# Where q of a later unit is asked for, and the order of one unit's attention, in a fused attention and feed-forward kernel

## The chip, the cores and the metric

The kernel runs on one core of a Trainium2 chip. The metric is the device time of one execution in microseconds. Before the change it is 909.99 us, the median of three runs (909.27 to 911.45).

## The reference

What is computed, with batch 8, 8 heads, 576 positions, 64 dimensions per head, and a feed-forward width of 2048:

```python
kv = np.einsum('bhsd,bhse->bhde', k, v)
out = np.einsum('bhsd,bhde->bhse', q, kv)
rms = np.sqrt(np.mean(out * out, axis=-1, keepdims=True) + 1e-06)
x = (out / rms * g_norm)            # then heads side by side: 4608 x 512
h = x @ w_in                        # 512 x 2048
r = np.maximum(h, 0.0)
g = s * (r * r) + b
return g @ w_out                    # 2048 x 512
```

All of it is in float32.

## The kernel before

**Units.** The 4608 rows of x are cut into 36 blocks of 128 rows, and four blocks make a unit; the code counts units from 0 to 8. In each unit the kernel multiplies the unit's x by `w_in` (`mm1`, or `mm1_deep` from unit 2 on), applies the activation, and multiplies by `w_out` (`mm2`). Both products use Winograd's form of the seven-product scheme for 2 x 2 blocks, at one or two levels. This needs sums and differences of blocks of x, of the weights and of the activations, which VectorE makes.

**Attention of the next unit.** While unit u is computed, the attention of unit u + 1 is made beside it, in two pairs of blocks, A and B. `attention_of_two` (L516) cuts each pair into steps: `turn` (VectorE transposes q, L540), `product` (64 or 32 small matmuls with k^T v on TensorE, L552), `back` (two VectorE transposes out of PSUM into the q tile, L564), `square` (ScalarE), `row_sum` (VectorE and ScalarE), `norm` (VectorE reads the q tile for the last time, L583 and L585), `turn_x` (VectorE, L596) and `scale` (ScalarE). `kv_product` (L365) makes k^T v of a batch: 144 matmuls, and four ScalarE copies (L400) into one of two tiles `bd_kv`. With its second argument true, it uses one PSUM bank each of the tags `z` and `y`; otherwise two of the tag `t`.

**The order is written out by hand.** The kernel schedules manually: each engine runs its instructions in the order in which the code emits them. In units 0 and 1, the second product is a list of slots, and `side_of` (L1628) says which steps follow which slot. In units from 2 on, `run` in `mm1_deep` (L947) calls `at(n)` between its pieces, and `sides` (L1718) gives two dictionaries: `first` for these places, and `second` for the places in `rest` (L1405) of `mm2`. At the beginning of `run` stand, in this order: `x1(0)`, `at(2)`, `x1(1)`, `sums_of_x` (four VectorE differences into two tiles of the pool `sub`), `small(2,0,1,2)`, `x6(0)`, `at(4)`, `at(5)`, `small(2,0,6,7)`, `y7(0)`, `at(6)`, `small(2,0,5)`. A `small` piece has short matmuls, each followed by a VectorE addition (L260 or L267) that reads the bank `sx_ps` or `z_ps`. The next matmul into `sx_ps` needs the addition before it.

**q tiles.** There are two of them (pool `qp`, two buffers). `load_q(c)` (L132) takes a tile for the pair of blocks c and c + 1 and returns the loads as a list; for the pair 14, the second half of unit 3, which is the fourth unit, it is 16 loads of 32 KB with runs of 32 floats. `loads` (L1651) issues them all at once on POOL's queue (L1655). A tile may be overwritten only after `norm` of the pair that it held.

**Weights and k, v.** SP loads pieces of the weights and of k and v into `ring`, 14 places of one tile, in the order of `queue_w2`; `used` frees places, and `pump` (L1063) then sends what fits. k and v of a unit stand ahead of its weights and take eight places.

**Stores of weight sums.** In unit 1, `parts_of_w` (L1130) makes the sums of each of the seven parts of `w_out` in tiles of the pool `sub` (six buffers, and two more for one of them) and stores them by four POOL DMAs (L1145) to `w3_dram`. These run in the even slots. Output stores (L1248) are on POOL too. So POOL's queue in the second half of unit 1 is: stores of parts 1, 2, 6, 7, 5; then 16 loads of q; then four output stores; stores of part 3; eight output stores; stores of part 4; four output stores.

The few lines that set this order before the change:

```python
            6: [B["norm"]],
            8: [B["turn_x"], B["scale"]],
            11: [sums],
            9: [partial(loads, 3, 1)],
```

## Time and profile before

| | us |
|---|---|
| median of three runs | 909.99 |
| the profiled execution | 909.79 |
| its span, from the first to the last instruction | 908.0 |
| PE busy (TensorE matmul) | 892.4 |
| DVE busy (VectorE) | 683.4 |
| ACT busy (ScalarE) | 345.5 |
| POOL busy (GpSimd) | 261.5 |

The durations in what follows come from the profiled execution. PE is a queue of 7662 matmuls; a matmul row's end is modelled, so the start of the next row tells more than a row's length. Idle time before an instruction is put down to the event that ended it. "w<-sub" is a store of weight sums from the pool `sub`; "w_sb" is the ring.

Of DMA, the page says: mean 208 GB/s over the span, and 188.77 MB in 121805 packets, of which 25456 are under 512 B. The second half of unit 1 runs from 181.37 us to 234.41 us of the span, unit 2 from there to 338.04 us.

### The profile page before, as it was taken

How to read it: one execution, taken by the hardware profiler on the slowest of the kernel's cores; microseconds unless marked ns; L12 is line 12 of the kernel's file. 1: busy time of each engine (PE TensorE's matmuls, PEld its weight loads, DVE VectorE, ACT ScalarE, POOL GpSimd, SP SyncE). 2: the span in 40 equal slices, each digit the busy share in tenths (PEclk: the TensorE clock that was granted, in tenths of full speed). 3: DMA queues.
4: the chain of work that ended last, by engine and by line, in shares of the span. 5: the costliest groups of instructions: out<-in, count | busy, mean ns of one | idle time of the engine just before them, and what ended most of it. 6: DMA issues, size and time to landing. Idle time of an engine off the chain costs nothing.

```text
span 908.0 us, 19742 instructions
## 1 busy us (share of the span) xinstructions
PE 892.4 (98%) x7662; PEld 825.4 (91%) x7662; DVE 683.4 (75%) x1321; ACT 345.5 (38%) x584; POOL 261.5 (29%) x493
## 2 busy tenths in 40 slices
PE   7999999999899999999999999999999999999998
PEld 6888888888789998999899989999999989999998
DVE  2899687785467986787678877796779777974696
ACT  2887024531057204640266026701661056204610
POOL 2027067023713415610473036503430200021000
PEclk9999999999999999999999999999999999999999
DMA  9897649359842996379735983498539921892186
GB/s 254 312 331 232 194 107 286 132 135 361 258 143 80 290 323 193 83 230 311 239 83 178 316 289 81 126 321 268 149 92 302 303 58 60 290 304 80 58 278 187
DMA packets 121805, 188.77 MB, mean 208 GB/s; under 512 B 25456, under 2 KB 43248, under 8 KB 121712
## 3 DMA queue, kind: packets, MB, share of 16 engines
q1 hardware_dynamic: 101744, 161.65, 55.1%
q0 software_dynamic: 16512, 23.63, 9.3%
q10 hardware_dynamic: 3456, 2.23, 1.0%
q8 instruction: 61, 1.00, 0.5%
q14 instruction: 32, 0.26, 0.1%
HBM read 160.70 MB, written 26.74 MB: 206 GB/s over the span
## 4 chain that ended last, share of the span: by engine, by line
PE 83%; DVE 6%; issue 4%; DMA 3%; POOL 2%; ACT 1%; SPq 0%; DVEq 0%; POOLq 0%
PE x_ps L92 40%; PE y_ps L92 22%; PE z_ps L92 10%; PE sx_ps L92 6%; PE st_ps L92 2%; PE y_ps L552 2%; DMA w<-sub 1%; POOL w L1145 1%; DMA kv_sb<-in_v_dram 1%; DMA q_sb<-in_q_dram 1%; PE kv_ps L384 1%; DVE sub L263 1%; PE z_ps L384 1%; DVE a L263 1%; POOL q_sb L1655 1%
## 5 line engine op out<-in xcount | busy, mean ns | idle before, releaser
L1655 POOL DMA_DIRECT2D q_sb<-in_q_dram x312 | 175.8, 571 | 127.1 <-issue 68.4
L1248 POOL DMA_DIRECT2D out_dram<-o x120 | 59.4, 502 | 324.9 <-issue 164.2
L92 PE MATMUL x_ps<-w_sb,sub 128*128 128x128 f32 x1176 | 148.8, 276 | 1.1 <-DVE r L260 1.0
L92 PEld LDWEIGHTS x_ps<-w_sb,sub 128*128 128x128 f32 x1176 | 139.7, 192 | 1.5 <-DVE r L260 1.5
L651 ACT ACTIVATE a<-a,b_col,s_col 128x512 f32<-128x512 f32 x144 | 116.9, 813 | 25.8 <-DVE a L654 17.6
L848 ACT COPY a<-x_ps 128x512 f32<-128x512 f32 x28 | 16.3, 581 | 232.0 <-PE x_ps L92 231.9
L92 PE MATMUL y_ps<-xs,wb 128*128 128x256 f32 x416 | 99.3, 382 | 0.0
L92 PE MATMUL x_ps<-xs,ws_raw 128*128 128x256 f32 x384 | 91.1, 380 | 0.1
L92 PEld LDWEIGHTS y_ps<-xs,wb 128*128 128x128 f32 x416 | 77.1, 192 | 9.2 <-issue 0.2
L92 PE MATMUL x_ps<-xT,wa 128*128 128x256 f32 x360 | 84.1, 382 | 0.1
L92 PEld LDWEIGHTS x_ps<-xs,ws_raw 128*128 128x128 f32 x384 | 70.1, 191 | 8.6 <-ACT r L725 0.5
L92 PEld LDWEIGHTS x_ps<-xT,wa 128*128 128x128 f32 x360 | 66.7, 190 | 10.6 <-ACT a L944 1.3
L944 ACT ACTIVATE a<-a 128x512 f32<-128x512 f32 x112 | 69.5, 620 | 5.5 <-DVE a L267 5.5
L92 PE MATMUL x_ps<-w_sb,a 128*128 128x128 f32 (+1 forms) x432 | 64.9, 299 | 0.0
L92 PE MATMUL y_ps<-w_sb,a 128*128 128x128 f32 (+1 forms) x416 | 62.2, 295 | 0.0
L92 PEld LDWEIGHTS x_ps<-w_sb,a 128*128 128x128 f32 x432 | 58.4, 192 | 2.9 <-issue 0.4
L92 PEld LDWEIGHTS y_ps<-w_sb,a 128*128 128x128 f32 x416 | 56.1, 192 | 2.1
L260 DVE TENSOR_TENSOR r<-sx_ps,a 128x256 f32<-128x256 f32 x84 | 35.1, 418 | 26.2 <-PE sx_ps L92 25.7
L260 DVE TENSOR_TENSOR r<-x_ps,o 128x256 f32<-128x256 f32 (+1 forms) x84 | 29.7, 353 | 27.7 <-PE x_ps L92 27.0
L92 PE MATMUL y_ps<-w_sb,sub 128*128 128x128 f32 x392 | 49.5, 275 | 0.0
L92 PE MATMUL z_ps<-w_sb,a 128*128 128x128 f32 (+1 forms) x352 | 46.9, 280 | 0.0
L263 DVE TENSOR_TENSOR a<-a,a 128x512 f32<-128x512 f32 x72 | 46.7, 684 | 0.1
(221 smaller groups left out, 1593.4 us busy)
## 6 DMA issues: line engine op xcount, KB each, us to landing
w_sb<-w SPq DMA_DIRECT2D x413, 256.0 KB, 4.8
w_sb<-w SPq DMA_DIRECT2D x14, 512.0 KB, 8.7
w<-sub POOLq DMA_DIRECT2D x28, 256.0 KB, 5.4
out_dram<-o POOLq DMA_DIRECT2D x112, 64.0 KB, 3.9
w_sb<-in_k_dram SPq DMA_DIRECT2D x24, 288.0 KB, 4.4
w_sb<-in_v_dram SPq DMA_DIRECT2D x24, 288.0 KB, 4.4
w_raw<-in_moe_w_in_dram SPq DMA_DIRECT2D x6, 1024.0 KB, 7.7
q_sb<-in_q_dram POOLq DMA_DIRECT2D x160, 32.0 KB, 3.2
```

The source lines that it names most:

```text
L92: nc.tensor.matmul(o, lhsT=lhsT, rhs=rhs, start=start, stop=stop, skip_group_check=True)
L260: nc.vector.tensor_tensor(out=o, in0=a, in1=b, op=ALU.add)
L263: nc.vector.tensor_tensor(out=o, in0=a, in1=b, op=ALU.subtract)
L384: nc.tensor.matmul(ps[r][(r ^ l) * HB : (r ^ l) * HB + HB, i, :], lhsT=kv[l][0][rows, j, :], rhs=kv[l][1][rows, j, :], start=(j == 0), sto ...
L552: nc.tensor.matmul(ps[l][32 * p : 32 * p + 32, r, lo:hi], lhsT=bd_kv[b % 2][rows, p, at : at + 32], rhs=st["qT"][rows, p, lo:hi], start=Tr ...
L651: nc.scalar.activation(t, t, AF.Identity, scale=s_col, bias=b_col)
L848: nc.scalar.copy(g_tile("a11", s), st["x", s])
L944: nc.scalar.square(ga[name, s], ga[name, s])
L1145: nc.gpsimd.dma_start(out=w3_dram[i][:, m - 4], in_=t)
L1248: queues[s % 2].dma_start(out=view[b, jj, :, cols], in_=st[name, j][s * w : s * w + w, cols])
L1655: load()
```

## The change

Two things are changed.

1. In unit 1, the sixteen loads of q for the pair 14 are not issued together after slot 9. They are issued in four lots of four, after slots 7, 8, 9 and 10. The tile is taken with the first lot.
2. In unit 2, the dictionary of its own is dropped, and the one of later units is used. k^T v moves from place 6 to place 2 and uses the `z` and `y` banks; A's `turn` moves from 4 to 2, A's `product` from 7 to 4, A's `back` and `square` and B's `turn` from 8 to 5, A's `row_sum` from 9 to 6, A's `norm` from 12 to 7, A's `turn_x` from 13 to 8, A's `scale` from 16 to 11. B's `back` stays at 11; B's `square` moves from 14 to 11, and `row_sum` from 15 to 12. B's `norm` and `turn_x` move from places 1 and 2 of the second half to 13 and 14 of the first, and B's `scale` from the place "sums" of the second half to 1. The loads of q for unit 4 move from 13 and from place 3 of the second half to 10 and 15.

```diff
+        pieces = []
+
+        def ask(n):
+            if n == 0:
+                pieces.extend(load_q(14))
+            for piece in pieces[4 * n : 4 * n + 4]:
+                piece()
+
         return {
             0: [A["scale"]],
             1: [B["turn"]],
             4: [B["product"], B["back"], B["square"]],
             5: [B["row_sum"]],
             6: [B["norm"]],
-            8: [B["turn_x"], B["scale"]],
+            7: [partial(ask, 0)],
+            8: [B["turn_x"], B["scale"], partial(ask, 1)],
+            9: [partial(ask, 2)],
+            10: [partial(ask, 3)],
             11: [sums],
-            9: [partial(loads, 3, 1)],
         }
...
-            kv.append(lambda: kv_product(kv_due[u], u > 2))
+            kv.append(lambda: kv_product(kv_due[u], u > 1))
...
-        if u == 2:
-            first = {
-                4: [A["turn"]],
-                6: kv,
-                7: [A["product"]],
-                8: [A["back"], A["square"], B["turn"]],
-                9: [A["row_sum"]],
-                10: [B["product"]],
-                11: [B["back"]],
-                12: [A["norm"]],
-                13: [A["turn_x"], *q[0]],
-                14: [B["square"]],
-                15: [B["row_sum"]],
-                16: [A["scale"]],
-            }
-            second = {1: [B["norm"]], 2: [B["turn_x"]], 3: [*q[1]], "sums": [B["scale"]]}
-        else:
...
+        first = {
+            2: [A["turn"], *(kv if u in (2, 5) else [])],
+            4: [A["product"], *(kv if u not in (2, 5) else [])],
+            5: [A["back"], A["square"], B["turn"]],
+            6: [A["row_sum"]],
+            7: [A["norm"]],
+            8: [A["turn_x"]],
+            10: [B["product"], *q[0]],
+            11: [B["back"], B["square"], A["scale"]],
+            12: [B["row_sum"]],
+            13: [B["norm"]],
+            14: [B["turn_x"]],
+            15: q[1],
+        }
+        second = {1: [B["scale"]]}
```

## The prediction

> **What bounds the kernel now.** I read the page first (PE busy 98% of the span, every other engine far below), then the table of PE's waits, because an engine at 98% can only gain where it waits or runs slow. Near unit 2 it names three waits:

> ```profile
> engine line waited for: us in total, times, longest us
> PE sx_ps L92 <- DVE r L260: 3.3, 1, 3.3
> PE y_ps L552 <- DVE qT L540: 1.1, 1, 1.1
> PE x_ps L92 <- DVE r L260: 1.0, 1, 1.0
> ```

> Each occurs once, though the code in question runs seven times. So I cut the span at the first matmul of each unit and asked for the windows of units 2 to 6 (columns: PE, PEld, DVE, ACT, POOL busy with counts, granted clock, DMA share, GB/s):

> ```profile
> 234.41:338.04 103.63, 98.16 (x917) 92.07 (x916) 73.47 (x151) 35.77 (x62) 33.16 (x62) 0.98 0.68 216
> 338.04:433.49 95.45, 95.45 (x887) 90.06 (x885) 74.91 (x153) 35.45 (x62) 35.01 (x66) 1.00 0.66 211
> 433.49:529.10 95.61, 95.61 (x918) 90.46 (x917) 74.91 (x153) 35.45 (x62) 34.98 (x66) 1.00 0.67 210
> 529.10:624.91 95.81, 95.73 (x919) 90.22 (x917) 74.60 (x153) 35.45 (x62) 35.00 (x66) 1.00 0.66 210
> 624.91:720.52 95.61, 95.61 (x918) 90.64 (x917) 74.90 (x153) 35.45 (x62) 26.83 (x50) 1.00 0.66 206
> ```

> All five do the same kinds of work, a k^T v product included, yet unit 2 takes 103.63 us and the others 95.45 to 95.81. Unit 2 alone runs below full clock. The excess of about 8 us is the whole prize. The timelines of DVE and POOL show where the first wait starts:

> ```profile
> 234.61 0.42 DVE L260 TENSOR_TENSOR o<-y_ps,or 128x256 f32<-128x256 f32 x1 [0.50 <-PE y_ps L92]
> 240.19 0.42 DVE L263 TENSOR_TENSOR sub<-xT 128x256 f32<-128x256 f32 x1 [5.15 <-DMA w<-sub]
> 242.75 0.42 DVE L263 TENSOR_TENSOR sub<-xT 128x256 f32<-128x256 f32 x1 [1.68 <-DMA w<-sub]
> 243.43 0.42 DVE L260 TENSOR_TENSOR r<-sx_ps,a 128x256 f32<-128x256 f32 x1
> ```

> ```profile
> 219.83 2.20 POOL L1145 DMA_DIRECT2D w<-sub  x4 [8.17 <-DVE sub L263]
> 222.03 2.91 POOL L1655 DMA_DIRECT2D q_sb<-in_q_dram  x5
> 225.89 0.58 POOL L1655 DMA_DIRECT2D q_sb<-in_q_dram  x1 [0.95 <-DMA w<-sub]
> 227.36 0.58 POOL L1655 DMA_DIRECT2D q_sb<-in_q_dram  x1 [0.89 <-DMA w<-sub]
> 228.54 5.23 POOL L1655 DMA_DIRECT2D q_sb<-in_q_dram  x9 [0.59 <-DMA w<-sub]
> 234.31 1.99 POOL L1248 DMA_DIRECT2D out_dram<-o  x4 [0.55 <-issue]
> 236.29 2.17 POOL L1145 DMA_DIRECT2D w<-sub  x4
> ```

> DVE stands still for 6.8 us because two of the six "sub" buffers are still being stored to w3_dram[3]; those stores were issued at 236.29 only, behind sixteen q loads that held POOL from 222.03 to 233.8. Then PE waits for DVE. What follows in PE's windows (the granted clock is the third figure from the right):

> ```profile
> 244.00:245.00 1.00, 1.00 (x5) 0.50 0.53 131
> 245.00:246.00 1.00, 1.00 (x6) 0.50 0.72 262
> 246.00:247.00 1.00, 1.00 (x3) 0.50 0.90 328
> 247.00:248.00 1.00, 1.00 (x5) 0.82 0.93 332
> 248.00:249.00 1.00, 1.00 (x43) 1.00 0.97 254
> ```

> The wait is paid twice: 3.3 us of idleness, then some 3.4 us at half clock, which costs another 1.7 to 1.9 us.

> [...] 3.26 us idle, then 0.50 until about 247.4. [...] q is read here in runs of 32 floats, 128 bytes. In the trace the sixteen loads of 32 KB of the next fetch, with little beside them, took 16.8% of sixteen engines over 14 us, so 2.35 us for 0.5 MB. [...] The trace has DMA shares of 0.9 to 1.08 from 205 to 230. I find no figure for the wait of a POOL load on an earlier one; the trace shows it (the waits on w<-sub in POOL's rows above).

> **The change part by part.**

> *q of the fourth unit.* No load is added or removed; sixteen move on POOL's queue. Each takes 0.58 us to issue. Lot 1 of four (2.3 us) goes behind w7's stores, which end at 211.66, into an idle stretch of 8.17 us. It needs the old tile free: the last reader, the norm at 210.56 + 1.23 = 211.8, is just done. So it runs 211.8 to 214.1 and w5's stores still start at 219.83. Lots 2 and 3 follow w5 as the first eight loads do now, with the same three waits, and end near 229.1. Then come the first output's four stores (0.5 each) to 231.1, and w3's stores 231.1 to 233.3, instead of 236.29 to 238.46: 5.2 us earlier. Lot 4 follows, to about 235.7. Behind it stand eight output stores and w4's four, which wait for earlier landings; I estimate w4 ending near 243 instead of 246.3; nothing in the next 20 us needs it. The third w3 store, issued near 232.2, lands near 237.5 with the 5.33 us that its landing takes now (chain of waits, 237.40). DMA time is unchanged; the quarter that moves into the busy stretch before 220 is 0.6 us of sixteen engines (a quarter of 2.35). That can delay k and v by at most that. No PE time is bought directly: it brings the two buffers about 5 us earlier.

> *k^T v first, in z and y banks.* 144 matmuls, 2.28 us on PE (248.38 to 250.65), move from behind y7(0) to behind x1(0), as in unit 5 (530.83 to 533.20 there). They fill most of the time in which PE waits now. New conditions: k and v in the ring by 236.14. The last is issued at 226.39 and such loads land in 4.4 to 7.0 us, so 231 to 233.4, and 234 with the 0.6 us above: covered by 2 us. z was last read at 195.8, the y buffer at 231.6: free. ACT's four copies (1.08 us) end near 239.7, before the z bank is wanted at 240.6 and bd_kv at 242.8. The ring's eight places come free 12 us earlier, so SP sends its waiting 256 KB loads earlier (it waits 14.2 us for kv_ps now); up to 2 MB, about 6 us at 330 GB/s, start at 238.5, beside w4's stores and perhaps lot 4. By then w3's have landed.

> *Attention in the order of later units.* Operations are kept, only their places move. DVE: A's transpose (1.24) now stands ahead of x's sums, 235.0 to 236.3, in time that was idle; the sums (four, some 1.5 us with gaps) run when the buffers are free, 237.5 to 239, and r follows sx at about 241.2. PE wants both at 244.05 (234.41 + 1.73 x1 + 2.30 kv + 1.73 x1 + 0.44 + 0.45 small + 1.82 x6 + 1.20 A's product = 244.08). So the 3.26 us wait goes, and the half clock with it. Even if w3 landed at 242.75 as today, r would end at 243.8, so this part is doubly covered. What is late next: between A's product and the small product 5, DVE runs back (2 x 0.65), B's transpose (1.20) and r (0.38); PE has only 2.7 us of work there. Unit 5 has just this and shows 0.24 us (542 region: y7 ends 541.49, next starts 541.73). I take 0.24 over. B's transpose at 245.4 needs lot 4, issued by 235.7; 6.6 us is the longest landing of such a load, so 242.3. B's product then lies where later units have it without a wait (1.13 us gone). B's norm and transpose leave the second half of the unit, where they hold up DVE just before the x_ps wait: 304.20 to 307.18 takes 2.98 against 1.79 in unit 3, and a further 0.22 at 315.4 goes. Their new place in the first half is the later units' one; DVE is as busy there. The q loads of unit 4 come earlier on a POOL that idles from 248.3 to 270.0; the memsets and stores behind them are 50 us away.

> *The sum.* New unit 2 = unit 5 (95.81), plus A's product of 64 instead of 32 matmuls (1.20 against 1.03: +0.17), less B's of 32 instead of 64 (-0.07) = 95.91. Saved: 103.63 - 95.91 = 7.72. Check by places: 3.33 + 1.86 half clock + 1.20 + 1.19 + 0.3 small = 7.88, less the 0.24 of unit 5 = 7.64. The profiled execution took 909.79 (span 908.0), so 902.07; the median lies 0.2 above it: 902.2. Bounds: nothing at all of 0.24 and unit 3's 95.45 as the floor gives -8.2; one new wait of 2.5 us without a clock drop gives -5.2.

> **Rivals.**
> 1. *A remnant wait takes over*: lot 4 is slowed by SP's earlier loads, and B's transpose stands at the head of DVE with r behind it. For: in-order DVE, DMA at 1.05 in 235 to 240. Against: nearly 10 us from issue to use. Landing at 249 costs 3.6 us plus about 1.8 of half clock: 902.2 + 5.4 = 907.6; at 247, 903.8.
> 2. *Slower: k and v are late.* PE would stand at 236.14 with nothing to pass it. The gain is used up when that wait reaches 5.9 us (5.9 + 1.8 half clock = 7.7), so if v lands after 242; at 244 the kernel takes 912. Against: that is 15.6 us from the issue at 226.39, and it was 7.0 at most in this stretch, though one store reached 13.0.
> 3. *The lots do nothing* (the DMAs, not POOL's order, set w3's landing): the second cover holds, 902.5. That is in the forecast's range. That the change doesn't do what it says is excluded by the emitted order: 4, 8 and 4 loads stand on POOL around w5 and w3, and k^T v behind the first x1.

> **How the numbers follow.** Forecast 0.81 (901.2 to 903.5, rival 3 within it); remnant wait 0.11 (903.5 to 908.1); about equal 0.03; k and v late, or an unforeseen wait of that size, 0.05. A measurement of this kernel tells 0.2%, 1.8 us, from no change. Faster 0.92, same 0.03, slower 0.05. Range 900.7 to 905.0: the spread of the three runs (909.27 to 911.45) below, half of rival 1 above.

> **What would show it.** Right: unit 2 in 95.7 to 96.5 us at clock 1.00; w3's stores on POOL near 231; no PE wait over 0.5 us in unit 2; kv rows at about 236.1 without a wait. Wrong: PE waiting for a DMA at kv, DVE waiting on q_sb at B's transpose near 245, or a new wait in the second half.

## The result, and the profile after

| | before | changed |
|---|---|---|
| median, us | 909.63 (909.08 to 911.45, 4 runs) | 904.46 (903.79 to 905.29, 4 runs) |
| ratio | | 0.994, 95% interval 0.9923 to 0.9958 |
| profiled execution, us | 909.79 | 905.29 |
| its span | 908.0 | 903.5 |
| unit 2, from its first matmul to unit 3's | 103.63 | 97.72 |

The kernel is 5.2 us faster where 7.7 were forecast. In the profiled executions, unit 2 is 5.91 us shorter, it starts 1.05 us later, and what stands behind it takes 0.36 us longer (570.32 against 569.96). Sum: -4.5 of the span. The kernel before has two kinds of executions: of the 58 that ran beside the experiments below, 13 had a mean granted clock of 0.999 or 1.000 and took 907.1 to 908.4 us, and the other 45, at a lower one, took 908.2 to 912.3.

None of the three waits near unit 2 of before is left in the table of PE's waits. These are the two lines that matter, and the second is new:

```profile
PE kv_ps L384 <- DMA kv_sb<-in_v_dram: 3.5, 2, 2.5
PE z_ps L92 <- issue: 1.6, 1, 1.6
```

The first is the wait for k and v at the very start of the kernel. It was 2.1 us in the profiled execution of before, and from 0.8 to 3.5 us in the traces of this study, whatever the kernel. So the later start of unit 2 comes from this wait and not from the change. The second is put down to "issue": PE waited for nothing that the profile names. It lies in unit 2. The window of unit 2 of the changed kernel (columns as in the prediction):

```profile
235.46:333.18 97.72, 96.10 (x918) 90.44 (x916) 73.73 (x151) 35.47 (x62) 31.09 (x58) 1.00 0.69 223
```

The clock is back to 1.00 in unit 2, and PE is idle there for 1.62 us (97.72 - 96.10). POOL's timeline of the changed kernel:

```profile
220.89 2.22 POOL L1145 DMA_DIRECT2D w<-sub  x4 [5.10 <-DVE sub L263]
223.09 2.92 POOL L1646 DMA_DIRECT2D q_sb<-in_q_dram  x5
...
230.46 1.99 POOL L1248 DMA_DIRECT2D out_dram<-o  x4
232.61 1.65 POOL L1145 DMA_DIRECT2D w<-sub  x3 [0.15 <-issue]
234.50 0.54 POOL L1145 DMA_DIRECT2D w<-sub  x1 [0.25 <-issue]
235.03 2.35 POOL L1646 DMA_DIRECT2D q_sb<-in_q_dram  x4
```

Part 3's stores start at 232.61; with the 1.05 us later start of unit 2 taken off that is 231.56, against 231.1 forecast. VectorE's timeline in the same stretch:

```profile
236.00 1.24 DVE L540 STREAM_TRANSPOSE qT<-q_sb 128x1024 f32<-128x1024 f32 x1
237.16 0.38 DVE L263 TENSOR_TENSOR sub<-xT 128x256 f32<-128x256 f32 x1
...
238.23 0.42 DVE L263 TENSOR_TENSOR sub<-xT 128x256 f32<-128x256 f32 x1 [0.22 <-DMA w<-sub]
...
242.10 0.42 DVE L260 TENSOR_TENSOR r<-sx_ps,a 128x256 f32<-128x256 f32 x1 [3.11 <-PE sx_ps L92]
```

The waits for the two buffers have shrunk from 6.8 us to 0.22, and VectorE now waits for PE where PE waited for it. Both the buffers and r came within 0.4 us of the forecast, once the later start is taken off. What is left is seen in PE's timeline:

```profile
241.83 0.28 PE L92 MATMUL z_ps<-xT,wa 128*128 128x128 f32 x1
243.72 0.60 PE L92 MATMUL z_ps<-xT,wa 128*128 128x128 f32 x3 [1.61 <-issue]
```

The pause falls between two rows of one small product (a row is one matmul record of the trace). A wait for a buffer or a bank should have held the first row already, as the 3.26 us of before stood ahead of all four rows of their product (243.90). So the question for the experiments was not only whether the mechanism of the forecast is right, but what this pause is.

A theory for it came from the DMA part of the page (packets, MB, share of the sixteen engines):

```profile
q8 instruction: 61, 1.00, 0.5%
```

PE has 7662 matmul rows, 7662 loads of weights and 397 other instructions in this trace, 15721 in all; 61 packets make 258 to a packet and 64 bytes to an instruction. The packets, of 16384 bytes each, start in step with PE: from the first to the last, one in 256 PE instructions on average. So q8 most likely carries PE's own program, 16 KB at a time; this is inferred from these counts and the queue's kind. Whether the 1.61 us are a wait for such a packet was to be shown. In the changed kernel, two packets near the pause stand unusually far apart:

```
changed kernel: packet at 214.71 us, next at 241.31 us: 520 PE instructions apart; k^T v is 288 of them
kernel before:  packet at 213.77 us, next at 239.12 us: 247 PE instructions apart
```

**Theory A**: the block of program behind k^T v was asked for when k^T v began, came late, and PE ran dry. **Theory B**, its rival: the `z` bank, which the change gave to k^T v, was not free.

### The profile page after: what moved, and what is told of

The parts are those of the page before. It is cut to its first block, busy times and chain, and to the rows that moved or that the text cites. A ratio compares the mean times of both kernels' runs of the same rounds, so it can differ in the third digit from the quotient of the medians.

```text
span 903.5 us, 19737 instructions
## 1 busy us (share of the span) xinstructions
PE 889.9 (98%) x7662; PEld 823.2 (91%) x7662; DVE 683.1 (76%) x1321; ACT 345.4 (38%) x584; POOL 262.5 (29%) x493
## 4 chain that ended last, share of the span: by engine, by line
PE 93%; DVE 3%; DMA 1%; issue 1%; ACT 0%; SPq 0%; POOL 0%; DVEq 0%
PE x_ps L92 46%; PE y_ps L92 25%; PE z_ps L92 10%; PE sx_ps L92 6%; PE st_ps L92 2%; PE y_ps L552 2%; DMA kv_sb<-in_v_dram 1%; PE z_ps L384 1%; PE kv_ps L384 1%; PE y_ps L384 0%; DVE xT L596 0%; DVE xn L585 0%; DVE xs L263 0%; DVE q_sb L564 0%; DVE qT L540 0%
## 5 line engine op out<-in xcount | busy, mean ns | idle before, releaser
L1665 POOL DMA_DIRECT2D q_sb<-in_q_dram x296 | 167.1, 573 | 86.1 <-issue 44.1
L1248 POOL DMA_DIRECT2D out_dram<-o x120 | 59.5, 503 | 360.3 <-issue 211.5
L92 PE MATMUL x_ps<-w_sb,sub 128*128 128x128 f32 x1176 | 148.5, 275 | 0.0
L92 PEld LDWEIGHTS x_ps<-w_sb,sub 128*128 128x128 f32 x1176 | 139.8, 192 | 0.0
L92 PE MATMUL y_ps<-xs,wb 128*128 128x256 f32 x416 | 98.5, 380 | 0.0
L92 PE MATMUL x_ps<-xs,ws_raw 128*128 128x256 f32 x384 | 91.1, 380 | 0.1
L92 PEld LDWEIGHTS y_ps<-xs,wb 128*128 128x128 f32 x416 | 76.3, 190 | 9.1 <-issue 0.2
L92 PE MATMUL x_ps<-xT,wa 128*128 128x256 f32 x360 | 84.3, 382 | 0.1
L92 PEld LDWEIGHTS x_ps<-xs,ws_raw 128*128 128x128 f32 x384 | 70.0, 190 | 8.7 <-ACT r L725 0.5
L92 PEld LDWEIGHTS x_ps<-xT,wa 128*128 128x128 f32 x360 | 66.5, 190 | 10.7 <-ACT a L944 1.7
L92 PE MATMUL x_ps<-w_sb,a 128*128 128x128 f32 (+1 forms) x432 | 64.9, 298 | 0.0
L92 PE MATMUL y_ps<-w_sb,a 128*128 128x128 f32 (+1 forms) x416 | 62.1, 295 | 0.0
L92 PEld LDWEIGHTS x_ps<-w_sb,a 128*128 128x128 f32 x432 | 58.4, 192 | 2.9 <-issue 0.4
L92 PEld LDWEIGHTS y_ps<-w_sb,a 128*128 128x128 f32 x416 | 56.1, 192 | 2.1
L260 DVE TENSOR_TENSOR r<-sx_ps,a 128x256 f32<-128x256 f32 x84 | 35.1, 418 | 24.6 <-PE sx_ps L92 24.1
L260 DVE TENSOR_TENSOR r<-x_ps,o 128x256 f32<-128x256 f32 (+1 forms) x84 | 29.6, 353 | 28.5 <-PE x_ps L92 27.8
L92 PE MATMUL y_ps<-w_sb,sub 128*128 128x128 f32 x392 | 49.5, 275 | 0.0
L92 PE MATMUL z_ps<-w_sb,a 128*128 128x128 f32 (+1 forms) x352 | 46.9, 280 | 0.0
L263 DVE TENSOR_TENSOR a<-a,a 128x512 f32<-128x512 f32 x72 | 46.7, 682 | 0.1
```

What stands on the lines that cost most here:

```text
L92: nc.tensor.matmul(o, lhsT=lhsT, rhs=rhs, start=start, stop=stop, skip_group_check=True)
L260: nc.vector.tensor_tensor(out=o, in0=a, in1=b, op=ALU.add)
L263: nc.vector.tensor_tensor(out=o, in0=a, in1=b, op=ALU.subtract)
L1248: queues[s % 2].dma_start(out=view[b, jj, :, cols], in_=st[name, j][s * w : s * w + w, cols])
L1665: load()
```

## The experiments

Times are medians, each against runs of the kernel before on the same chip (its medians there 909.4 to 910.1). "Unit 2" is cut from the profile as above.

**1. The lots alone.** Unit 2's dictionary and banks as before, with the four lots.

```diff
-            8: [B["turn_x"], B["scale"]],
+            7: [partial(ask, 0)],
+            8: [B["turn_x"], B["scale"], partial(ask, 1)],
+            9: [partial(ask, 2)],
+            10: [partial(ask, 3)],
             11: [sums],
-            9: [partial(loads, 3, 1)],
```

> The change's first part alone: q of the fourth unit in four lots, the second unit's attention in its old order. w3's stores leave POOL some 4 to 5 us earlier, so x's differences no longer hold DVE until 243 us. Theory 1 (the late buffers were the cause of the first wait, half clock its consequence): the 3.26 us wait on PE and the half clock after it go, about 5.1 us; the 1.1 us wait before B's product and the 1.2 us of the second half stay; 904.5. Rival (the place of k^T v decides, lots do nothing): 909.6 as before.

Measured: 904.53 us, ratio 0.9944 (0.993 to 0.9958). Unit 2 takes 98.44 us, 5.19 less than before, which is exactly 3.33 + 1.86, the wait with the half clock of the forecast's check by places. The waits of PE that are left are the two that this part leaves alone:

```profile
PE y_ps L552 <- DVE qT L540: 1.1, 1, 1.1
PE x_ps L92 <- DVE r L260: 1.0, 1, 1.0
```

So the late buffers caused the first wait, and the half clock, which followed that wait, goes with it (the granted clock of unit 2 is 1.00 here).

**2. The order alone.** All sixteen loads after slot 9 as before, unit 2 in the later order.

```diff
-            7: [partial(ask, 0)],
-            8: [B["turn_x"], B["scale"], partial(ask, 1)],
-            9: [partial(ask, 2)],
-            10: [partial(ask, 3)],
+            8: [B["turn_x"], B["scale"]],
             11: [sums],
+            9: [partial(loads, 3, 1)],
```

> The second part alone: all sixteen q loads after slot 9 as before, the third unit's attention and k^T v in the later order. Prediction's step 'doubly covered': with k^T v in front and w3 landing near 242.8, r ends at 243.8 and PE wants it at 244.05, so the time is that of the whole change without what the lots buy: 904.5, at most 0.4 more. Rival (the lots carry the first wait's gain): PE waits again 2 us or more before the small product 6, or DVE waits for q at B's transpose, and the time is 906.5 to 908.

Measured: 903.36 us, ratio 0.9931 (0.9916 to 0.9945): 1.1 us less than expected, and than the whole change. VectorE still waits 5.84 us for the stores (6.83 before), yet PE waits for none of it:

```profile
241.44 0.43 DVE L263 TENSOR_TENSOR sub<-xT 128x256 f32<-128x256 f32 x1 [5.42 <-DMA w<-sub]
...
242.74 0.43 DVE L263 TENSOR_TENSOR sub<-xT 128x256 f32<-128x256 f32 x1 [0.42 <-DMA w<-sub]
```

The second cover of the forecast holds here, but barely. The addition r ends at 243.84; PE would have wanted it at 243.91 (the unit's start at 234.24, plus the forecast's 9.67) had it not paused. The pause is there too, at the same row, with 0.79 us instead of 1.61. The parts save 5.19 and 6.74 us of unit 2 alone and 5.91 together: they remove the same wait, each by itself. With the lots the pause was longer in every trace (1.59 to 1.65 us in experiments 3, 4 and the changed kernel, against this one trace without them).

**3. Other banks.**

```diff
-            kv.append(lambda: kv_product(kv_due[u], u > 1))
+            kv.append(lambda: kv_product(kv_due[u], u > 2))
```

> The whole change, but k^T v of the second unit in two banks of tag t instead of z and y. In the trace of the changed kernel PE stood still for 1.61 us inside the small product 2, whose bank is z. Theory A (the instruction fetch of PE came late: one 16 KB fetch started at 241.31 when 520 instructions had run since the last instead of about 256): the pause stays or moves by less than 0.5 us, time 904.5 within 0.5. Theory B (the z bank, read by ScalarE's copies of k^T v, was not free): the pause goes, 902.9.

Measured: 903.71 us (0.9936, 0.992 to 0.9951). The pause is at the same row, 1.59 us, behind a packet at 240.01. Theory B falls. The time is 0.75 us below the whole change's, half of what theory B asked for, but the pause has not become shorter. In the profiled executions of this kernel and of experiment 4, 0.36 of 0.58 us lie before unit 2 (it starts at 234.20 and 234.56), so most of it is the start of the kernel.

**4. The changed kernel again**, unedited.

> The changed kernel once more, for a second trace. If the pause inside the small product 2 comes from the program (its place in PE's instruction stream), it is there again, at the same matmul, 1 to 2 us long, and unit 2 takes 97.5 to 98 us. If it was an accident of that one execution, unit 2 takes 95.9 to 96.2 us and the median falls to 903 in more than half of the rounds.

Measured: 904.48 us; the pause is 1.65 us at the same row, and unit 2 takes 97.76 us. So the pause belongs to the program.

**5 and 6. Sixteen small matmuls more at the start**, in the whole change and in the order alone. Nothing near unit 2 is edited; PE's later instructions only move up by 64 places in its stream.

```diff
         for _ in range(n):
             matmul(ps[:, 0, :P], ident, ident, True, True)
+        if n == 7:
+            for _ in range(16):
+                matmul(ps[:8, 1, :8], ident[:, :8], ident[:, :8], True, True)
```

> The changed kernel with sixteen more warm-up matmuls of 8 x 8 behind the second warm-up of the first k^T v: some 64 more PE instructions (each such matmul is two loads of weights and two matmul rows), at most 1 us of time at the start, where PE waits for k and v by 0.8 to 1.8 us in most traces. They shift every later 16 KB boundary of PE's instruction stream: the fetch that comes due with the first matmuls of k^T v of unit 2 comes due before x1(0). Theory A (the fetch falls due inside k^T v's burst of 288 instructions in 2.3 us): the pause of 1.6 us in the small product 2 goes, unit 2 takes 95.9 to 96.3 us, the time is 903.0. Rival (the pause belongs to this place, whatever stands before it: a wait that the trace doesn't name): the pause stays, 97.5 to 98 us, time 904.5 to 905.5.

> The order part alone with the same sixteen small matmuls. Theory A: its pause of 0.8 us goes as well; unit 2 in 96 us, time 902.6. If the lots have a use of their own once the pause is gone, this is slower than the whole change with the shift by 0.3 us or more; if not, the two are equal within 0.3 us.

Measured: 907.17 us (0.9979, 0.9971 to 0.9988) and 908.61 us (0.999, 0.9975 to 1.0004). Both times were missed by 4 us and more, in the wrong direction. But the pause in unit 2's small product is gone in both; unit 2 of the first takes 95.85 us. Other pauses have come in its stead. The longest of the first kernel is in unit 4:

```profile
438.51 0.21 PE L387 MATMUL y_ps<-w_sb 64*64 64x64 f32 x1 [1.08 <-issue]
```

and that of the second is in unit 5:

```profile
534.50 0.92 PE L92 MATMUL x_ps<-xT,wa 128*128 128x256 f32 x3 [1.74 <-issue]
```

There is a shorter one in unit 3 of the first (0.47 us) and one in unit 4 of the second (1.39 us). All are at or just behind a k^T v, and each kernel has one more, of 1.2 and 1.5 us, in the first k^T v of all. With it, unit 2 starts at 236.00 and 237.48, where the other kernels of the experiments start it at 233.81 to 234.56; where the rest of that delay comes from stays open. Counted in PE instructions from the start, the four pauses of these two kernels in units 3, 4 and 5 are before instructions 5825, 7617, 7617 and 9410; the pause of the changed kernel is before 3778. The distances to 3778 are 2047, 3839 and 5632, which are 8, 15 and 22 times 256 within one. The pause in the first k^T v, before instruction 450, lies on the same lines. The places fit a fixed grid of 256 instructions. That PE pauses where a line of the grid is reached before its packet has been taken in is inferred from these places and from the starts of the packets below. Such a pause cost up to 1.74 us in these two kernels.

Unit 2 of the second kernel takes 97.09 us, 1.2 more than that of the first: without the lots, PE waits there 1.0 us for VectorE, which waits for part 3's stores. The first kernel, with the lots, is also 1.4 us faster in the median, to which its shorter pauses contribute.

**7. Eight ring loads left out.** The first eight loads into the places that k and v leave.

```diff
+            if left_out and left_out[0]:
+                left_out[0] -= 1
+                ...
+                continue
```

> The changed kernel without the first eight ring loads into the places that k and v of unit 2 leave (2 MB from 238.5 us on): the weights of those eight pieces are wrong, so unit 2's rows are not the reference's; all instructions of PE are there. Contention theory (the 16 KB fetch waits behind data on full DMA engines): the fetch starts by 239.5 instead of 240 to 241.3, the pause in the small product 2 is under 0.5 us. Rival (the fetch is asked for late, or can't be taken while k^T v runs at 125 instructions per us): start at 240 or later and pause over 1.2 us though the engines are freer. One look.

Measured, in one execution: unit 2 takes 97.17 us. The packet starts at 238.97, 3.1 us after it is asked for, and the pause is 1.06 us, between the two expectations. In the changed kernel these loads are issued from 238.47 on, 1 us after the packet is asked for, so they were the wrong ones to take away: without them the DMA share is still 0.98 in the 4 us from k^T v's start. This is inconclusive by itself; experiment 12 does it better.

**8. k^T v in two halves**, with x1(1) between them.

```diff
             x1(1)
+            at(3)
             sums_of_x()
...
+                kv.append(lambda: kept.append(kv_product(3, False, (0,))))
...
+                rest = [lambda: kv_product(3, False, (1,), kept[0])]
```

> The changed kernel with k^T v of unit 2 in two halves of 72 matmuls: one behind x1(0), one behind x1(1), in two banks of tag t. PE uses up 144 instructions at a stretch instead of 288, with 1.7 us of x1(1) between. Theory A: the pause falls to 0.5 us or less, since the fetch has that time as well; time 903.2. Rival (only the fetch's start counts, which full DMA engines set): fetch at 240 to 241.3 again, and a pause of 1.2 to 1.6 us at the same matmul; 904.3.

Measured: 903.75 us (0.9936, 0.9921 to 0.9951), but a pause of 1.80 us, unit 2 99.82 us in the profiled execution. The expectation of theory A failed: the packet started at 240.69, 4.3 us after it was asked for, though PE used its instructions up less fast. So the burst alone is not it; the start of the packet counts, too. In this execution the pause was followed by half clock, for 3.41 us from 243.22 on (columns: length, PE busy, clock, DMA share, GB/s):

```profile
243.00:244.00 1.00, 0.84 (x4) 0.61 1.05 402
244.00:245.00 1.00, 1.00 (x3) 0.50 1.02 348
```

**9 to 11. Fewer PE instructions at the start.** The 25 warm-up matmuls of 128 columns are done as wider ones with the same 3200 columns: 8 matmuls in 9 and 10 (68 PE instructions less), 21 in 11 (16 less). Experiment 9 has the whole change, 10 and 11 the order alone. The edit of 9 and 10:

```diff
-        for _ in range(n):
-            matmul(ps[:, 0, :P], ident, ident, True, True)
+        for k in (4, 2, 1):
+            for _ in range(n // 4 if k == 4 else (n & k) // k):
+                matmul(
+                    ps.rearrange("p a (b n) -> p (a b) n", n=P)[:, :k], ident,
+                    ident.unsqueeze(1).to_broadcast((P, k, P)), True, True,
+                )
```

> The changed kernel with the 25 warm-up matmuls of 128 columns at the start done as 8 wider ones of the same 3200 columns in all: 68 PE instructions fewer, so that the 16 KB boundaries of PE's stream come 68 instructions later. By the traces so far a block of 256 instructions is asked for about 28 instructions before the block ahead of it is entered, and k^T v is in danger when that point falls on its first 45 instructions or just before (33 in the changed kernel's unit 2; 22, -5 and 16 in units 3, 4, 5 of the kernels with sixteen more small matmuls, which paused there). With 68 less, it falls on 101, 154, 127, 148 and 201 in units 2 to 6. Theory A: no pause over 0.5 us put down to issue anywhere behind the start, unit 2 in 95.9 to 96.3 us, time 902.8. Rival (the pauses of the shifted kernels came from something else about the added matmuls): a pause of 1 us or more in unit 2 stays; 904.5.

> The order part alone with the same eight wide warm-up matmuls. Theory A: no pause, unit 2 in 95.9 to 96.3 us, 902.6, equal to the whole change with them within 0.3 us: the lots then buy nothing. If the lots do help once the pause is gone: slower than the whole change by 0.3 us or more, with a wait for w3's stores or for q in unit 2.

> The order part alone with four warm-up matmuls fewer (the same columns): 16 PE instructions less, so that the asking point falls on instruction 49 of unit 2's k^T v instead of 33. A block then has about 5.9 us instead of 4.3 until its first instruction is wanted, against 5.3 that the fetch took in the order part's trace. Theory A: no pause or one under 0.3 us in unit 2. Rival as before: 0.8 us. One look.

Measured: 902.11 us (901.73 to 902.38; ratio 0.9916, 0.9902 to 0.993); 903.52 us (902.24 to 906.62; 0.9933, 0.9917 to 0.9949); and 901.82 us in one execution. No trace of the three has a wait put down to issue. The window of unit 2 in experiment 9 (columns: length, PE busy with its count, clock, DMA share, GB/s):

```profile
234.04:329.95 95.91, 95.90 (x918) 1.00 0.70 228
```

This is the 95.91 us that the forecast's sum had for unit 2, and it starts no earlier than in the other kernels (234.04). Unit 2 takes 95.85 us in experiment 11 and 96.73 in experiment 10: there part 3's stores landed later still, and the second cover did not quite hold. VectorE's second wait in experiment 10, and PE's two waits behind it:

```profile
243.63 0.42 DVE L263 TENSOR_TENSOR sub<-xT 128x256 f32<-128x256 f32 x1 [1.12 <-DMA w<-sub]
```

```profile
244.78 0.71 PE L92 MATMUL sx_ps<-sub,w_sb 128*128 128x128 f32 x4 [0.49 <-DVE r L260]
...
248.00 0.71 PE L92 MATMUL sx_ps<-sub,w_sb 128*128 128x128 f32 x4 [0.21 <-DVE r L260]
```

So where unit 2 has no pause, the lots are worth 0 to 1.2 us of it, by how the stores happen to land (experiments 11, 10 and 6). The medians of experiments 9 and 10 are 1.4 us apart, like those of 5 and 6: the expectation that the lots buy nothing failed, and its alternative came. Experiment 9 is the version that beats both kernels; its five executions all lie below the ten of the changed kernel here and in experiment 4 (903.76 to 906.76).

**12. Freer DMA engines.** Unit 1's output stores and the first fourteen ring loads of unit 2's weights left out; PE's instructions in the changed kernel's places.

```diff
+            if u == 1:
+                return
...
+            if u == 2 and left_out[0]:
+                left_out[0] -= 1
+                ...
+                continue
```

> The changed kernel without unit 1's output stores and without the first fourteen ring loads of unit 2's weights (six before k^T v, eight behind it): unit 1's rows stay unwritten and unit 2's rows are wrong; PE's instructions are all there. The 16 KB block that comes due at instruction 33 of unit 2's k^T v should meet DMA engines that are mostly free. Contention theory: the fetch starts 1.0 to 1.5 us after it is asked for, as in units 3, 4 and 6 (DMA share 0.4 to 0.6, 1.0 us), instead of 3.8 us; the block is used 3.4 us after the asking, before the 4.3 us that PE needs to get there, so no pause. Rival (the fetch is slow there for another reason than full engines): start 2.5 us or more after the asking and a pause of 0.8 us or more. One look.

Measured, in one execution: there is no pause, and unit 2 takes 95.84 us. The packet starts at 238.20, 1.9 us after the asking at about 236.3, between the two expectations; the engines were free only from 238 on (columns: length, PE busy, clock, DMA share, GB/s):

```profile
236.00:237.00 1.00, 1.00 (x63) 1.00 0.85 307
237.00:238.00 1.00, 1.00 (x83) 1.00 0.93 320
238.00:239.00 1.00, 1.00 (x32) 1.00 0.46 164
```

The start at the moment of relief, and 1.9 us instead of 3.8, speak for full engines as what holds the packet back. This is one execution, and it does not tell the engines from the memory behind them.

The packets and pauses together, from the traces' packets and PE's rows, in us. "Asked" is an inference. Where PE is slow, a packet appears about 28 instructions before a grid line (in the changed kernel, of the 24 packets that start where PE runs at most 14 instructions per us, 17 start 13 to 38 before one); and the pauses, with their packets, are explained if that packet holds the block behind the next line, so that it is asked for 284 instructions ahead.

```
kernel, unit            asked    packet starts   later by   PE goes on   after packet's start
changed, 2              237.5      241.31          3.8        243.72        2.41
other banks, 2          236.3      240.01          3.7        242.43        2.42
again, 2                236.6      240.34          3.7        242.86        2.52
order alone, 2          236.3      239.31          3.0        241.67        2.36
eight loads less, 2     235.9      238.97          3.1        241.52        2.55
halves, 2               236.4      240.69          4.3        243.16        2.47
shifted, 3              339.2      340.20          1.0        343.08        2.88
shifted, 4              434.8      436.06          1.3        438.51        2.45
order shifted, 4        436.9      438.00          1.1        440.91        2.91
order shifted, 5        529.3      532.04          2.8        534.50        2.46
freer engines, 2        236.3      238.20          1.9        (no pause)
```

## Why the prediction was right, and where it fell short

- *The excess of unit 2 is the prize, and its first wait comes from part 3's stores*: shown by experiment 1, 5.19 us by that alone.
- *Half clock follows the wait and goes with it*: shown for the profiled executions, 5.19 is wait and half clock together. The 13 executions of before with a mean clock of 0.999 or 1.000 speak for a half clock that does not follow every time. How long a wait has to be for it, the runs do not show. In the kernel before, 3.26 us of idleness were followed by 3.41 us at 0.50, and in experiment 8, 1.80 us by 3.41 us of half clock; in the changed kernel, 1.61 us in unit 2 left the clock at 1.00, and so did the 2.47 us for v at the start (1.00 in every window from 4 to 16 us). That the forecast has no half clock for a new wait of 2.5 us (its bound of -5.2) or of 1.6 us (rival 1 at 247) was an estimate.
- *The lots bring the stores about 5 us earlier*: right; with the later start of 1.05 us taken off, 231.56 for a forecast of 231.1. (Part 4's stores end at 245.9 in the same reckoning, for an estimate of 243; nothing waited for them.) *No PE time is bought directly*: beside the new order the lots add little, 0 to 1.2 us of unit 2, and in the changed kernel they go with a longer pause (1.61 and 1.65 us, against 0.79 without them).
- *Doubly covered*: nearly. In experiment 10, r ends at 244.73 where PE wants it at 244.06 (the unit's start at 234.39, plus 9.67), and PE lost 0.70 us.
- *k and v in time, banks free, B's transpose not held up by lot 4*: right. There is no wait of k^T v for DMA in unit 2 in any of these traces. That the moved loads could delay k and v, by at most 0.6 us, was an estimate; no run measured such a delay. *B's product and the second half of the unit lose their waits*: right, none is left.
- *What is late next: 0.24 us of the later units*: here the forecast fell short, by an omitted term. "New unit 2 = unit 5 (95.81), plus ... = 95.91" took over unit 5's PE time for the same order. Experiment 9 (95.91) and experiment 11 (95.85) show that the sum holds where there is no pause. It left out that the move of k^T v to an earlier place also moves it against the grid of PE's program, where unit 2 has a line 61 instructions into the 288 and engines at a DMA share of 1.00 to 1.11 (238 to 242 us). That costs 1.6 us here, of 1.8 us that unit 2 is over the forecast. Most of the 2.3 us between 902.2 and 904.46 is this; the rest is the start of the kernel, within its spread.
- The rivals: a new wait of the size of the remnant wait (1) is what came (903.8 to 907.6 was its range), but by another mechanism than lot 4. k and v late (2) did not happen. That the lots do nothing (3) is refuted by experiment 1.
- The range, 900.7 to 905.0, held because half of rival 1 had been added above. The result lies outside the 901.2 to 903.5 that had a chance of 0.81. So the direction and the mechanism of the saving were right, and that the range covers the loss was luck. Of the four signs of being right, two came (the stores near 231, k^T v at 236.2 without a wait, both with the 1.05 us taken off), and two did not: unit 2 took 97.72 us, and PE has a wait over 0.5 us in it.

What stays open: why a packet of 16 KB starts up to 4.3 us after the inferred asking, and why not always. Experiment 12, and in part experiment 7, show a shorter delay with freer engines (1.9 and 3.1 us, against 3.8 and 3.7 in the two traces of the changed kernel), not how the packet is queued; in unit 5 of experiment 5 it was only 1.3 us at a DMA share of 1.02, and in unit 5 of the changed kernel 1.2 us at 1.08 (526 to 528 us).

## What to carry to other kernels

When a trace shows one pass of a repeated stage longer than its siblings, cut all of them and take the best sibling as the target: here the sum made from it came within 0.1 us of the unit without a pause. A move of a dense run of small matmuls is also a move in PE's instruction stream; after it, look for a wait put down to issue right behind the run. Where one is found, a change in the number of earlier PE instructions (here 68 fewer, in the warm-up) can remove it, and can also put another one elsewhere (64 more took the pause out of unit 2 and put others of 0.47 to 1.74 us into units 3, 4 and 5), so all such runs of the kernel have to be read again in a new trace.

## What the hardware showed that was not expected

From a packet's start until PE went on, 2.36 to 2.91 us passed in the ten pauses of the table. Of this the packet itself took 0.9 to 1.5 us; after its end came another 1.3 to 1.6 (1.14 and 1.27 in unit 2 of the changed kernel). Before its start, counted from the inferred asking, came 1.0 to 1.3 us in the table's units 3 and 4, and 1.9 to 4.3 us in its units 2 and 5. In the changed kernel it was 0.8 and 0.9 us in units 3 and 4, with a DMA share of 0.50 and 0.59 (340 to 342 and 435 to 437 us), and 3.8 us in unit 2, with 1.03 (237 to 241 us). In the changed kernel PE took 1.8 us for 256 instructions at the quickest, in a k^T v, and 10 to 25 us in 78% of all such stretches.

So in these traces such a run paused only where a packet was asked for near its beginning, by the same inference. Leaving the first k^T v aside, there was no pause with the asking point on instruction 42 of the run or later, in any trace. With it between -5 and 33 there was one in ten of fourteen cases: not at 151 us in experiment 11 (-2), in unit 5 of experiment 5 (16), in unit 3 of experiment 6 (22), nor with the freer engines of experiment 12 (33). There is no case between 33 and 42.
